# Attention over 32 memory slots, then a cosine feed-forward network: score and float32 fold products of 64x32 in two PSUM banks, the first batch's keys loaded ahead of its values, and a written order of issue

## The chip, the cores and the metric

The kernel runs on one core of a Trainium2 chip. The metric is the device time of one execution in microseconds. Before the change it is 708.84 us, the median of 3 runs (708.61 to 710.9).

## The reference

There are 8 batches of 576 tokens with 8 heads of 64. Per head, `phi` is turned by a softmax over the tokens into weights that gather keys and values into 32 memory slots; each token attends over the 32 slots; the heads side by side are a row of 512 that goes through the feed-forward network (4608 rows of 512, `w_in` 512 by 2048, `w_out` 2048 by 512).

```python
a = phi - np.max(phi, axis=2, keepdims=True)
a = np.exp(a)
a = a / (np.sum(a, axis=2, keepdims=True) + 1e-09)
k_m = np.einsum('bhsm,bhsd->bhmd', a, k)
v_m = np.einsum('bhsm,bhsd->bhmd', a, v)
scores = scale * np.matmul(q, k_m.transpose(0, 1, 3, 2))
scores = scores - np.max(scores, axis=-1, keepdims=True)
attn = np.exp(scores)
attn = attn / (np.sum(attn, axis=-1, keepdims=True) + 1e-09)
return np.matmul(attn, v_m).astype(np.float32)
...
h = x @ w_in
g = h * np.cos(h)
return (g @ w_out).astype(np.float32)
```

The weights come in as 64-bit floats and are turned into float32 on the chip.

## The kernel before

**Tiling.** The 4608 tokens are 12 groups of 384 (`GT`); two batches of 576 make three groups. The inner size 2048 is 16 chunks of 128 (`NF`). The main loop has 12 x 16 steps. In each, `gemm1` multiplies a chunk's folded weight with a group's attention rows into a PSUM tile `hp`; `act` and `act_end` make h*cos(h) of it on ScalarE and VectorE (L544 to L559); `gemm2` adds its product with the chunk of `w_out` to three PSUM tiles `acc`, four steps later (`LAG`).

**The attention is folded into the weights.** `x @ w_in` is attention times (`v_m` times `w_in`), so for each batch a *fold* multiplies `vm` (the 32 value slots of each head) with `w_in`, 256 rows by 2048 columns, and `gemm1` has an inner size of 256 in place of 512. `fold_first` (batch 0) and `fold` with `b < 2` (batch 1) do so in float32 from `w_in_sb`; from batch 2 on `fold_psum` uses half-precision high and low parts (`vp`, `vl`, `w2`), made in group 1.

**Precision.** Group 0 multiplies in float32 (L524, L572). From group 1 on each product is three half-precision ones, high x high, high x low and low x high (L533: 6 products of 384 columns, or 12 of 192 where a group spans two batches; L577: 9 of 512).

**Batch preparation.** `prep(b)` is `memory(b)` and then `attend(b)`, a generator advanced a step at a time beside the main loop. `memory` takes the softmax of `phi` and sums keys and values into `psA` (L270: 32-column tiles, `kv` chunks of at most 128 tokens with a column of ones for the denominators), divides (L283 to L287), turns the result around (`tpx`, L292) and copies it to `km` and `vm` (L299 to L302). Both are kept with zeros between two heads, filled by GpSimd, so one product of 128 rows by 64 columns serves two heads:

```python
nc.tensor.matmul(sc[D * p:D * (p + 1), g * n:(g + 1) * n], lhsT=km[:, 2 * g + p],
                 rhs=qt[:, 2 * g + p, t0:t0 + n], start=True, stop=True)
```

`attend` makes the scores in blocks of tokens (`BLK`: 256, 256, 64; batch 0: 256, 128, 192), one PSUM tile `sc` of the small pool a block (`score_products`), transposes each out on VectorE in 32x32 squares (`score_back`, L381), and takes the softmax (L389 to L400, the exponential on ScalarE, L422).

**PSUM.** Eight banks: three for `acc` (`ps_acc`), three for `hp` (`ps_h`), two for everything else (`ps_s`, `small_ps`): scores, folds, `psA`, `tpx`.

**The start.** Loads go out on SyncE's queue in program order: `phi`, all of batch 0's `kv`, the first 384 tokens of `q`, then the weight pieces (`load_w_in`, `load_w_out`). `to_float32` turns a piece into float32: VectorE takes the sign (L143), ScalarE the low exponent bits and a scaling (L147, L151), VectorE joins them (L152), ScalarE squares for the scale (L154). Between the first products stand `warm` products on zeros (L630), which nobody reads. During group 0 one piece is turned per step, and `fold_first` follows each piece of `w_in`.

**Order of issue.** A scheduler in the framework orders each engine's instructions from its own cost estimates; `tc.keep_in_program_order` pins single ones.

## Time and profile before

| | us |
|---|---|
| median of 3 runs | 708.84 (708.61 to 710.9) |
| the profiled execution | 710.08 |
| its span | 708.3 |
| mean granted TensorE clock | 0.994 of full speed |

The profiled execution is one run of its own; its span is what the rows of the profile cover. A row of the list of groups names the line, the engine, the operation, output <- input with their shapes and the count, then busy time and the mean of one instruction in ns, then the idle time just before them and what ended most of it. A timeline row has the start, the duration, the engine, the line and the operation, with the wait ahead of it in brackets. A product's tile is written rows*columns (128*64), its operands partitions x elements. In windows the rows have the window and its length, then each engine's busy time and instructions (TensorE's products, TensorE's weight loads, VectorE, ScalarE, GpSimd), the granted clock, the share of the DMA engines and GB/s.

### The profile page before, as it was taken

To read this page: it belongs to the slowest core of one execution; us is meant where nothing else is said; L and a number is where in the kernel's file an instruction comes from. 1 tells how busy PE (TensorE), PEld (TensorE's weight loads), DVE (VectorE), ACT (ScalarE), POOL (GpSimd) and SP (SyncE) were. 2 spreads that over 40 slices of the span, in tenths; PEclk is the share of its full clock that TensorE was granted. 3 is DMA by queue.
4 is the path that set the end of the run, shared out by engine and by line. 5 is a ranking of instruction groups with operands and counts; after the bars stand their busy time and mean duration, and the time that the engine had idled before them with its cause. 6 is when DMAs were issued, how large, how long until landed. Compare 5 with 4: busy or idle time off the path is not lost.

```text
span 708.3 us, 11822 instructions
## 1 busy us (share of the span) xinstructions
PE 687.8 (97%) x4597; PEld 364.7 (51%) x4597; DVE 532.7 (75%) x1135; ACT 518.7 (73%) x951; POOL 13.7 (2%) x34
## 2 busy tenths in 40 slices
...
GB/s 281 379 321 218 266 293 60 105 61 195 146 1 237 44 1 1 56 226 1 44 1 167 99 16 1 46 206 31 44 2 2 22 23 1 46 1 1 45 1 44
DMA packets 31959, 66.18 MB, mean 93 GB/s; under 512 B 2208, under 2 KB 12320, under 8 KB 31904
## 3 DMA queue, kind: packets, MB, share of 16 engines
...
## 4 chain that ended last, share of the span: by engine, by line
PE 60%; DVE 21%; ACT 16%; DMA 2%; issue 1%; ACTq 0%; POOL 0%; DVEq 0%; SPq 0%
PE acc L577 33%; PE hp L533 16%; DVE u L547 4%; ACT u L552 3%; DVE u L556 3%; DVE gp L559 3%; PE psA L270 3%; DVE vw L478 2%; PE sc L376 2%; PE pv L471 2%; ACT gp L558 2%; DMA phi<-in_phi 2%; DVE wo L191 2%; PE hp L524 1%; DVE w_in_parts L202 1%
## 5 line engine op out<-in xcount | busy, mean ns | idle before, releaser
L577 PE MATMUL acc<-wo,gp 128*128 128x512 f16 x1584 | 371.8, 379 | 1.2 <-DVE ob L589 0.7
L577 PEld LDWEIGHTS <-gp 128*128 128x128 f16 x1584 | 153.3, 98 | 162.6 <-issue 4.1
L533 PE MATMUL hp<-aT,vw 128*128 128x192 f16 (+1 forms) x1440 | 202.7, 284 | 1.0 <-DVE u L556 1.0
L533 PEld LDWEIGHTS <-vw 128*128 128x128 f16 x1440 | 128.3, 98 | 77.4 <-issue 17.5
L552 ACT ACTIVATE u<-u,quarter 128x384 f32<-128x384 f32 x192 | 116.7, 615 | 63.8 <-DVE u L547 62.9
L556 DVE SCALAR_TENSOR_TENSOR u<-hp,u 128x384 f32<-128x384 f32 x176 | 96.5, 553 | 60.6 <-ACT u L552 60.1
L544 ACT ACTIVATE gp<-hp,cu 128x192 int32<-128x192 f32 (+1 forms) x240 | 115.4, 492 | 28.1 <-PE hp L533 12.3
L547 DVE SCALAR_TENSOR_TENSOR u<-hp,cu,gp 128x192 f32<-128x192 f32 (+1 forms) x240 | 118.8, 503 | 21.9 <-ACT gp L544 21.5
L559 DVE TENSOR_TENSOR gp<-u,gp 128x384 f16<-128x384 f32 x176 | 96.4, 552 | 43.0 <-ACT gp L558 41.9
L558 ACT CAST gp<-u 128x384 f16<-128x384 f32 x176 | 88.8, 510 | 54.3 <-DVE u L556 53.0
L572 PE MATMUL acc<-wo,gp 128*128 128x512 f32 x96 | 45.1, 599 | 0.0
L478 DVE SCALAR_TENSOR_TENSOR vw<-pv,vw 128x512 f16<-128x512 f32 x48 | 31.5, 684 | 3.0 <-ACT vw L477 2.9
L524 PE MATMUL hp<-aT,vf 128*128 128x384 f32 x64 | 25.6, 533 | 7.9 <-DVE vf L497 3.1
L477 ACT ACTIVATE vw<-pv 128x512 f16<-128x512 f32 x48 | 26.8, 589 | 1.1 <-PE pv L471 0.9
L572 PEld LDWEIGHTS acc<-wo,gp 128*128 128x128 f32 x96 | 17.4, 190 | 17.8 <-issue 15.2
L601 ACT ACTIVATE ob<-acc,os 128x512 f32<-128x512 f32 x27 | 17.8, 682 | 9.6 <-PE acc L577 7.1
L524 PEld LDWEIGHTS hp<-aT,vf 128*128 128x128 f32 x64 | 12.2, 202 | 20.1 <-issue 4.3
L552 ACT ACT_TABLE_LOAD x17 | 21.8, 1283 | 0.3
L270 PE MATMUL psA<-kv,phi 128*32 128x129 f32 (+1 forms) x640 | 21.0, 275 | 0.7 <-ACT phi L260 0.5
L376 PE MATMUL sc<-q,km 128*64 128x256 f32 (+3 forms) x192 | 19.8, 342 | 1.6 <-DVE vw L478 1.2
L270 PEld LDWEIGHTS psA<-kv,phi 128*32 128x32 f32 (+1 forms) x640 | 16.4, 109 | 7.3 <-issue 3.3
L376 PEld LDWEIGHTS sc<-q,km 128*64 128x64 f32 x192 | 12.1, 140 | 12.0 <-issue 3.6
...
## 6 DMA issues: line engine op xcount, KB each, us to landing
...
```

The source lines that it names most:

```text
L270: nc.tensor.matmul(psA[32 * j:32 * (j + 1), g * KV:(g + 1) * KV], lhsT=a[:n, c, h * M:(h + 1) * M], rhs=kvs[c][:n, h * KV:(h + 1) * KV], s ...
L376: nc.tensor.matmul(sc[D * p:D * (p + 1), g * n:(g + 1) * n], lhsT=km[:, 2 * g + p], rhs=qt[:, 2 * g + p, t0:t0 + n], start=True, stop=True)
L478: nc.vector.scalar_tensor_tensor(out=vw[:, 1, g], in0=src, scalar=T, in1=vw[:, 0, g], op0=ALU.mult, op1=ALU.subtract)
L533: nc.tensor.matmul(hp[:, c0:c0 + n], lhsT=vw[:, wi, g, fo * P:(fo + 1) * P], rhs=aT[:, ai, g, c1:c1 + n], start=(k == 0), stop=(k == 5))
L544: ins = nc.scalar.activation(ni[:, c], hp[:, c], AF.Copy, scale=cu, bias=0.25)
L547: nc.vector.scalar_tensor_tensor(out=u[:, c], in0=hp[:, c], scalar=cu, in1=ni[:, c], op0=ALU.mult, op1=ALU.subtract)
L552: nc.scalar.activation(u, u, AF.Sin, scale=TWO_PI_BELOW, bias=quarter)
L556: nc.vector.scalar_tensor_tensor(out=u, in0=hp[:, :GT], scalar=2.0 ** -17, in1=u, op0=ALU.mult, op1=ALU.mult)
L558: nc.scalar.copy(gp[:, 0], u)
L559: nc.vector.tensor_tensor(out=gp[:, 1], in0=u, in1=gp[:, 0], op=ALU.subtract)
L572: nc.tensor.matmul(accs[grp][t], lhsT=gp[:, t * P:(t + 1) * P], rhs=wo[:, f + 1], start=(f == 0), stop=(f == NF - 1))
L577: nc.tensor.matmul(accs[grp][t], lhsT=gp[:, gi, t * P:(t + 1) * P], rhs=parts[:, wi], start=(f == 0 and gi == 0 and wi == 0), stop=(f == N ...
```

## The change

`km` and `vm` lose their zeros: 32 columns a head. A block of scores becomes eight products of 64 rows by 32 columns, four heads on rows 0 to 63 into one bank and four on rows 64 to 127 into another; the blocks become 288 and 288 tokens (batch 0: 384 and 192), and two transposes take a block out. The float32 folds get the same form (`fold_single`), and `fold_first` copies one bank on ScalarE and one on VectorE. For batch 0 the host lays out keys (with the ones) and values apart; `memory_first` loads keys ahead of `q` and the first weight piece, values behind it, and sums, turns and copies the keys before the values. There are 43 warm products (before: 51). `NEXT` is a table with the position, among the instructions not yet issued, of the next one on each engine; `issue_in_order` makes each engine keep it. The pins go.

```diff
+K1 = D + 1
...
-BLK = [(0, 256), (256, 256), (512, 64)]
-BLK_FIRST = [(0, 256), (256, GT - 256), (GT, S - GT)]
+BLK = [(0, 288), (288, 288)]
+BLK_FIRST = [(0, GT), (GT, S - GT)]
...
+NEXT = {
+    mybir.EngineType.PE: (
+        "0x16 2x2 0x16 1x8 0x11 8 16x3 0x19 1 2 3 0x4 4 0x29 18x2 0x20 1 0x3 2x6 0x3 7x2 0x3 1 19x2 2 0x5 1 "
...
+    mybir.EngineType.SP: (
+        "0x34 6x2 0 5x2 0x2 3 0 2 0x5 16 0 1 0x3 1 0x3 1 0x3 1 0x2 2 0x7 2x2 0x6 2x2 0x6 2x2 0x6 2x2 0x12 "),
+}
+
+
+def issue_in_order(tc):
+
+
+    traced = [i for i in tc.nc.cur_bb.bb.instructions if not type(i).__name__.startswith("BassTile")]
+    for engine, text in NEXT.items():
+        left = [i for i in traced if i.engine == engine]
+        last = None
+        for word in text.split():
+            at, _, times = word.partition("x")
+            for _ in range(int(times or 1)):
+                ins = left.pop(int(at))
+                if last is not None:
+                    tc.add_manual_dep(ins, last.name, mybir.DependencyInfo(
+                        mybir.DependencyClass.NoSync, mybir.DependencyReason.DATA), reason="issue order")
+                last = ins
+        assert not left, engine
...
+    def load_first(src, c0, c1):
+        if c0 == 0:
+            loads["kv", 0] = [ld.tile([P, H * KV], F32, tag="kv", name=f"kv_0_{c}", bufs=5) for c in range(5)]
+        for c, (s0, n) in enumerate(TCH):
+            nc.sync.dma_start(out=loads["kv", 0][c][:n, c0:c1], in_=src[s0:s0 + n])
...
+        psk = small_ps("psk")
+        for c in range(5):
+            products(psk, c, 0, K1)
+            yield
...
+        tpx = small_ps("tpx_k")
+        for g in range(2):
+            nc.tensor.transpose(tpx[:, g * P:(g + 1) * P], X[:, g], ident)
+        lo, hi = slice(0, D), slice(D, P)
+        tv = tpx[:, 0:HM].rearrange("p (c t m) -> p c t m", t=2, m=M)
+        km = wk.tile([P, NP, M], F32, tag="km", name=f"km_{b}", bufs=1)
+        nc.scalar.mul(km[lo], tv[lo, :, 0], 1.0 / math.sqrt(D))
+        nc.vector.tensor_scalar(out=km[hi], in0=tv[hi, :, 1], scalar1=1.0 / math.sqrt(D), scalar2=None, op0=ALU.mult)
+        st["km", 0] = km
+        psv = ps_acc.tile([P, DM], F32, tag="ps_acc", name="psv")
+        for c in range(5):
+            products(psv, c, H * K1, D)
+            if c == 2:
+                yield
+        X = wk.tile([P, 2, P], F32, tag="back", name="X_v", bufs=4)
+        for g in range(2):
+            nc.scalar.activation(X[:, g].rearrange("p (t d) -> p t d", t=2),
+                                 psv[:, g * D:(g + 1) * D].unsqueeze(1).broadcast_to([P, 2, D]), AF.Copy,
+                                 scale=den[:, g:g + 1])
+        tpx = ps_acc.tile([P, DM], F32, tag="ps_acc", name="tpx_v")
+        for g in range(2):
+            nc.tensor.transpose(tpx[:, g * P:(g + 1) * P], X[:, g], ident)
+        tv = tpx[:, 0:HM].rearrange("p (c t m) -> p c t m", t=2, m=M)
+        vm = wk.tile([P, NP, M], F32, tag="vm", name=f"vm_{b}")
+        nc.scalar.copy(vm[hi], tv[hi, :, 0])
+        nc.scalar.copy(vm[lo], tv[lo, :, 1])
+        st["vm", 0] = vm
...
-        km = wk.tile([P, NP, 2 * M], F32, tag="km", name=f"km_{b}", bufs=1)
-        vm = wk.tile([P, NP, 2 * M], F32, tag="vm", name=f"vm_{b}")
-        nc.gpsimd.memset(km, 0.0)
-        nc.gpsimd.memset(vm, 0.0)
+        km = wk.tile([P, NP, M], F32, tag="km", name=f"km_{b}", bufs=1)
+        vm = wk.tile([P, NP, M], F32, tag="vm", name=f"vm_{b}")
         tv = tpx[:, 0:HM].rearrange("p (c t m) -> p c t m", t=2, m=M)
         lo, hi = slice(0, D), slice(D, P)
-        nc.scalar.mul(km[lo, :, 0:M], tv[lo, :, 0], 1.0 / math.sqrt(D))
-        nc.scalar.mul(km[hi, :, M:2 * M], tv[hi, :, 1], 1.0 / math.sqrt(D))
-        nc.vector.tensor_copy(out=vm[hi, :, 0:M], in_=tv[hi, :, 0])
-        nc.vector.tensor_copy(out=vm[lo, :, M:2 * M], in_=tv[lo, :, 1])
+        nc.scalar.mul(km[lo], tv[lo, :, 0], 1.0 / math.sqrt(D))
+        nc.scalar.mul(km[hi], tv[hi, :, 1], 1.0 / math.sqrt(D))
+        nc.vector.tensor_copy(out=vm[hi], in_=tv[hi, :, 0])
+        nc.vector.tensor_copy(out=vm[lo], in_=tv[lo, :, 1])
...
-            sc_at[i] = sc = small_ps(f"sc_{b}_{t0}")
-            for g in range(2):
-                for p in range(2):
-                    nc.tensor.matmul(sc[D * p:D * (p + 1), g * n:(g + 1) * n], lhsT=km[:, 2 * g + p],
-                                     rhs=qt[:, 2 * g + p, t0:t0 + n], start=True, stop=True)
+            sc_at[i] = sc = [small_ps(f"sc_{b}_{t0}_{g}") for g in range(2)]
+            for c in range(NP):
+                for g in range(2):
+                    rows = slice(g * D, (g + 1) * D)
+                    nc.tensor.matmul(sc[g][M * c:M * (c + 1), :n], lhsT=km[rows, c],
+                                     rhs=qt[rows, c, t0:t0 + n], start=True, stop=True)
 
         def score_back(i):
             t0, n = BL[i]
-            nc.vector.transpose(at[:, 2 * t0:2 * (t0 + n)], sc_at[i][:, :2 * n])
+            for g in range(2):
+                nc.vector.transpose(at[:, 2 * t0 + g * n:2 * t0 + (g + 1) * n], sc_at[i][g][:, :n])
...
-        score_products(0)
-        score_products(1)
-        score_back(0)
-        score_back(1)
-        yield
-        score_products(2)
-        score_back(2)
+        scores(0)
+        yield
+        scores(1)
...
     def fold_psum(b, q, g):
         pv = small_ps(f"pv_{b}_{q}_{g}")
-        for i in range(2):
-            c = 2 * g + i
-            if b < 2:
-                nc.tensor.matmul(pv[D * i:D * (i + 1)], lhsT=st["vm", b][:, c],
-                                 rhs=w_in_sb[:, c, q * FS:(q + 1) * FS], start=True, stop=True)
-        if b >= 2:
-            for first in (True, False):
-                for j in range(4):
-                    c, o = 2 * g + j // 2, 1 - j % 2
-                    nc.tensor.matmul(pv[M * j:M * (j + 1)], lhsT=(st["vp", b] if first else vl)[:, c, o],
-                                     rhs=st["w2", q][:, c, o], start=first, stop=not first, skip_group_check=True)
+        for first in (True, False):
+            for c in range(NP):
+                nc.tensor.matmul(pv[M * c:M * (c + 1)], lhsT=(st["vp", b] if first else vl)[:, c, 1 - g],
+                                 rhs=st["w2", q][:, c, 1 - g], start=first, stop=not first, skip_group_check=True)
+        return pv
+    def fold_single(b, name, c0, n):
+        pv = [small_ps(f"{name}_{g}") for g in range(2)]
+        for c in range(NP):
+            for g in range(2):
+                rows = slice((1 - g) * D, (2 - g) * D)
+                nc.tensor.matmul(pv[g][M * c:M * (c + 1), :n], lhsT=st["vm", b][rows, c],
+                                 rhs=w_in_sb[rows, c, c0:c0 + n], start=True, stop=True)
         return pv
...
-        for g, pv in enumerate([fold_psum(b, q, g) for g in range(2)]):
-            split_fold(b, vw, g, pv)
+        pv = fold_single(b, f"pv_{b}_{q}", q * FS, FS) if b < 2 else [fold_psum(b, q, g) for g in range(2)]
+        for g in range(2):
+            split_fold(b, vw, g, pv[g])
 
     def fold_first(j):
         q, r = divmod(j, 2)
         if r == 0:
             st["vf", q] = wk.tile([P, 2, FS], F32, tag="vw", name=f"vf_{q}", bufs=8)
-        pv = small_ps(f"pvf_{j}").rearrange("p (g x) -> p g x", g=2)
-        for g in range(2):
-            for i in range(2):
-                c = 2 * g + i
-                nc.tensor.matmul(pv[D * i:D * (i + 1), g], lhsT=st["vm", 0][:, c],
-                                 rhs=w_in_sb[:, c, j * WS:(j + 1) * WS], start=True, stop=True)
-        (nc.scalar.copy if j < 2 else nc.any.tensor_copy)(out=st["vf", q][:, :, r * WS:(r + 1) * WS], in_=pv)
+        pv = fold_single(0, f"pvf_{j}", j * WS, WS)
+        nc.scalar.copy(out=st["vf", q][:, 0, r * WS:(r + 1) * WS], in_=pv[0][:, 0:WS])
+        nc.vector.tensor_copy(out=st["vf", q][:, 1, r * WS:(r + 1) * WS], in_=pv[1][:, 0:WS])
...
-    load_kv(0)
+    load_first(k_first, 0, H * K1)
     load_q(0)
     load_w_in(0)
+    load_first(v_first, H * K1, H * KV)
...
-        warm((1, 1, 2, 2, 0)[c])
+        if c < 4:
+            warm(1)
     next(mem)
     warm(3)
-
-    def attention_rest(sign):
-        tc.keep_in_program_order(sign)
-        next(mem)
-        warm(2)
-
-    convert_w_in(0, attention_rest)
-    for _ in mem:
-        pass
+    next(mem)
+    convert_w_in(0)
     first = attend(0)
     next(first)
-    warm(12)
+    warm(4)
+    next(mem)
+    warm(2)
+    next(mem)
+    next(mem)
+    warm(2)
     fold_first(0)
     warm(6)
     next(first)
+    for _ in mem:
...
+        pass
...
+    issue_in_order(tc)
...
+        "k_first": np.concatenate([kt[0], np.ones((S, H, 1), k.dtype)], axis=2).reshape(S, H * K1),
+        "v_first": np.ascontiguousarray(vt[0]).reshape(S, H * D),
```

Three places show what the table and the rest move. First TensorE at batch 2's scores, late in group 1: `sc_2_0` and the like are score blocks of batch 2 (after: with the bank's number behind), `acc_1` and `hp_2` are main products of groups 1 and 2, `32x288 x4` are four products into a 32-row strip each. Before, the first two blocks and, 28 rows on, the third:

```order
L577 LDWEIGHTS gp_1_13_1395
L577 MATMUL acc_1_2_1032<-wo_87,gp_1_13_1395 128x512
L376 MATMUL sc_2_0_1633<-q_2_659,km_2_1587 64x256 x4
L376 MATMUL sc_2_256_1638<-q_2_659,km_2_1587 64x256 x4
L533 LDWEIGHTS vw_1_0_780
```

```order
L577 MATMUL acc_1_2_1032<-wo_87,gp_1_14_1431 128x512
L577 LDWEIGHTS gp_1_14_1431
L577 MATMUL acc_1_2_1032<-wo_87,gp_1_14_1431 128x512
L376 MATMUL sc_2_512_1669<-q_2_659,km_2_1587 64x64 x4
L533 LDWEIGHTS vw_1_0_780
```

and after the change:

```order
L749 MATMUL acc_1_1_1133<-wo_87,gp_1_14_1541 128x512
L556 MATMUL sc_2_0_0_1741<-q_2_741,km_2_1697 32x288 x4
L749 LDWEIGHTS gp_1_14_1541
L749 MATMUL acc_1_2_1134<-wo_87,gp_1_14_1541 128x512
L556 MATMUL sc_2_0_1_1742<-q_2_741,km_2_1697 32x288 x4
L749 LDWEIGHTS gp_1_14_1541
L749 MATMUL acc_1_2_1134<-wo_87,gp_1_14_1541 128x512
L749 LDWEIGHTS gp_1_14_1541
L749 MATMUL acc_1_2_1134<-wo_87,gp_1_14_1541 128x512
L556 MATMUL sc_2_288_0_1777<-q_2_741,km_2_1697 32x288 x4
L707 LDWEIGHTS vw_1_0_874
```

The first block's two banks now stand apart, with a product of group 1 between them, and one bank of the second block follows after two more.

Then VectorE at the start, from the division of batch 0's sums on: `den`, `X` and `l1` are of `memory`, `at`, `rm` and `rs` of the first score blocks, `w_in_sb`, `raw_in` and `wo` of the weight pieces. Before:

```order
L283 TENSOR_SCALAR den_0_203<-psA_0_156 128x2
L284 RECIPROCAL den_0_203<-den_0_203 128x2
L287 TENSOR_SCALAR X_0_206<-psA_0_156,den_0_203 128x128 x2
L306 TENSOR_REDUCE l1_0_230<-X_0_206 128x4
L308 TENSOR_TENSOR l1_0_230<-l1_0_230,vmask_78 128x4
L310 TENSOR_REDUCE l2_0_233<-l1_0_230 128x1
L301 COPY vm_0_217<-tpx_0_213 64x4x32
L302 COPY vm_0_217<-tpx_0_213 64x4x32
L164 TENSOR_SCALAR ev_0_237<-l3_0_235 128x1
L165 TENSOR_SCALAR ev_0_237<-ev_0_237 128x1
L381 STREAM_TRANSPOSE at_0_241<-sc_0_0_244 128x512
L381 STREAM_TRANSPOSE at_0_241<-sc_0_256_250 128x256
```

and after:

```order
L253 TENSOR_SCALAR w_in_sb_86<-raw_in_0_106 128x4x256
L375 TENSOR_SCALAR den_0_206<-psk_161 128x2
L376 RECIPROCAL den_0_206<-den_0_206 128x2
L379 TENSOR_SCALAR X_k_209<-psk_161,den_0_206 128x128 x2
L259 SCALAR_TENSOR_TENSOR w_in_sb_86<-raw_in_0_106,w_in_sb_86 128x4x256
L390 TENSOR_SCALAR km_0_218<-tpx_k_215 64x128
L562 STREAM_TRANSPOSE at_0_227<-sc_0_0_0_230 128x384
L562 STREAM_TRANSPOSE at_0_227<-sc_0_0_1_231 128x384
L570 TENSOR_REDUCE rm_0_228<-at_0_227 128x24
L571 TENSOR_TENSOR at_0_227<-at_0_227,rm_0_228 128x768
L253 TENSOR_SCALAR w_in_sb_86<-raw_in_1_113 128x4x256
L575 TENSOR_REDUCE rs_0_229<-at_0_227 128x24
```

The first piece's sign (L253, before L143) has moved ahead of the division and its join (L259, before L152) ahead of the copy of `km`; the values' part (`l1`, `vm`) has left the stretch ahead of the scores.

Last ScalarE at the start, from its first weight piece on. Before (`km` is copied ahead of it, `vf` are copies of folds):

```order
L299 ACTIVATE km_0_216<-tpx_0_213 64x4x32
L300 ACTIVATE km_0_216<-tpx_0_213 64x4x32
L147 ACTIVATE w_in_sb_86<-raw_in_0_106 128x4x256
L151 ACTIVATE raw_in_0_106<-raw_in_0_106 128x1024
L422 ACTIVATE at_0_241<-at_0_241 128x768
L147 ACTIVATE w_in_sb_86<-raw_in_1_108 128x4x256
L154 ACTIVATE raw_in_0_106,sq_90<-w_in_sb_86 128x1024
L497 COPY vf_0_268<-pvf_0_269 128x2x256
```

and after:

```order
L257 ACTIVATE w_in_sb_86<-raw_in_0_106 128x4x256
L258 ACTIVATE raw_in_0_106<-raw_in_0_106 128x1024
L389 ACTIVATE km_0_218<-tpx_k_215 64x128
L261 ACTIVATE raw_in_0_106,sq_90<-w_in_sb_86 128x1024
L257 ACTIVATE w_in_sb_86<-raw_in_1_113 128x4x256
L400 ACTIVATE X_v_289<-psv_246,den_0_206 128x128
L603 ACTIVATE at_0_227<-at_0_227 128x768
L400 ACTIVATE X_v_289<-psv_246,den_0_206 128x128
L258 ACTIVATE raw_in_1_113<-raw_in_1_113 128x1024
L408 COPY vm_0_295<-tpx_v_292 64x128
L409 COPY vm_0_295<-tpx_v_292 64x128
```

The first piece (L257, before L147) now comes ahead of `km`, its square (L261, before L154) ahead of the exponential, and the values' products are divided and copied here (L400, L408, L409).

125 lines of the change are left out of this document (81 added, 44 removed), and 74 rows, old and new, of the table NEXT.

## The prediction

> **What bounds the kernel now.** I read the page first, then busy time by stage, then single stretches of TensorE's timeline. The page's first lines, and the three narrow product groups that the change rewrites:
>
> ```profile
> span 708.3 us, 11822 instructions
> PE 687.8 (97%) x4597; PEld 364.7 (51%) x4597; DVE 532.7 (75%) x1135; ACT 518.7 (73%) x951; POOL 13.7 (2%) x34
> L577 PE MATMUL acc<-wo,gp 128*128 128x512 f16 x1584 | 371.8, 379 | 1.2 <-DVE ob L589 0.7
> ```
> ```profile
> L376 PE MATMUL sc<-q,km 128*64 128x256 f32 x120 | 14.7, 385 | 0.3 <-POOL l L312 0.3
> L495 PE MATMUL pvf<-w_in_sb,vm 128*64 128x256 f32 x64 | 9.6, 422 | 2.2 <-DVE w_in_sb L152 2.1
> L465 PE MATMUL pv<-w_in_sb,vm 128*64 128x512 f32 x32 | 7.7, 605 | 0.0
> ```
>
> TensorE is busy 97% of the span, but that is an average over two stages. Busy time by stage (the window, its length, then PE, PEld, DVE, ACT, POOL):
>
> ```profile
> 18.70:110.00 91.30, 81.19 (x371) 39.27 (x368) 77.85 (x150) 87.10 (x123) 1.99 (x6) 0.96 0.82 282
> 110.00:150.00 40.00, 39.27 (x234) 21.38 (x233) 39.81 (x82) 37.91 (x78) 0.31 (x1) 1.00 0.29 74
> 150.00:250.00 100.00, 99.33 (x733) 53.22 (x731) 89.32 (x198) 78.39 (x144) 2.71 (x6) 1.00 0.39 121
> 250.00:350.00 100.00, 99.19 (x748) 55.60 (x747) 72.10 (x162) 71.01 (x142) 2.37 (x5) 1.00 0.17 58
> 350.00:450.00 100.00, 98.38 (x660) 50.43 (x659) 72.24 (x150) 68.63 (x127) 2.87 (x4) 1.00 0.15 50
> 450.00:550.00 100.00, 99.99 (x793) 55.53 (x791) 75.64 (x177) 73.06 (x141) 2.09 (x4) 1.00 0.18 59
> 550.00:650.00 100.00, 99.82 (x669) 55.13 (x668) 70.33 (x144) 70.51 (x140) 0.00 (x0) 1.00 0.05 17
> ```
>
> Up to 110 us ScalarE sets the pace: 87.1 of 91.3 us busy, 4.2 idle. From 150 us on it is TensorE: 500 us long, idle for 0.67+0.81+1.62+0.01+0.18 = 3.3 us in all. In that stage a microsecond of TensorE work is a microsecond of time, and 3.3 us is about all that a better order can win back.
>
> **TensorE's prices** come from its timeline (start, duration, what):
>
> ```profile
> 468.67 0.40 PE L471 MATMUL pv<-w_in_sb,vl 128*32 128x512 f16 x4
> 469.00 1.16 PE L533 MATMUL hp<-aT,vw 128*128 128x192 f16 x12
> 470.00 1.03 PE L577 MATMUL acc<-wo,gp 128*128 128x512 f16 x4
> 471.04 1.95 PE L376 MATMUL sc<-q,km 128*64 128x256 f32 x16
> 472.92 1.25 PE L577 MATMUL acc<-wo,gp 128*128 128x512 f16 x5
> 474.10 0.45 PE L376 MATMUL sc<-q,km 128*64 128x64 f32 x8
> 474.49 1.16 PE L533 MATMUL hp<-aT,vw 128*128 128x192 f16 x12
> 475.49 2.11 PE L577 MATMUL acc<-wo,gp 128*128 128x512 f16 x9
> 477.43 1.15 PE L533 MATMUL hp<-aT,vw 128*128 128x192 f16 x12
> ```
>
> Durations overlap, so I take start to start. Nine full-width products of 512 half-precision columns take 477.43-475.49 = 1.94 us, 0.216 each. A float32 product is two records, and each record of 256 columns streams as long: four logical products per block, two 64-column halves side by side, two blocks, so 8 rounds of 0.216 = 1.73 us. The row says 1.88 (471.04 to 472.92): 0.15 goes at leaving. The five products ahead of the second visit take 1.18 instead of 5 x 0.216 = 1.08: 0.10 goes at entering. So each visit of TensorE to a narrow shape costs about 0.25 us beside its streaming. The start shows the same for the very shape that the change brings, 64 rows by 32 columns:
>
> ```profile
> 14.11 0.61 PE L630 MATMUL warm<-zeros 128*128 128x512 f16 x2
> 14.65 0.64 PE L270 MATMUL psA<-kv,phi 64*32 64x129 f32 x16
> 15.22 0.82 PE L630 MATMUL warm<-zeros 128*128 128x512 f16 x3
> ```
>
> From 14.11 to 15.22 is 1.11 us: two warm products (0.43), 16 records of 129 columns on four column tiles (4 rounds of 0.216 x 129/256 = 0.109, so 0.44), and 0.24 for the visit.
>
> **Scores.** If all eight 64x32 products of a block run side by side, a block of 288 columns is two records of 0.243, 0.49 us, and a batch 0.97 in two visits, 1.47 with them. Before it is 1.88 + 0.39 (474.10 to 474.49) + two entries of 0.10 = 2.46. For the six batches 2 to 7, which lie in TensorE's stage, blocks kept whole would save 6 x 0.99 = 5.9 us. But the table does not keep them whole. Counted in the order listing from the first product of group 1 to the end, the scores of batches 2 to 7 make 20 visits (before: 12), each one round of 0.49, since no visit holds a tile twice: 20 x (0.49 + 0.25) = 14.8, against 6 x 2.46 = 14.8 before. **The scores save nothing.** In batch 5 the second block alone makes three visits, of one, two and five products.
>
> **Folds.** Batch 1's last three float32 folds: before, 3 visits of 2 rounds of 0.86 (512 columns, two records of 0.43): 3 x (1.73+0.25) = 5.9. After, 7 visits of one round: 7 x (0.86+0.25) = 7.8, so +1.9. The half-precision folds keep their products, but their visits rise from 25 to 31: +1.5, and one fold cut 5 to 11 adds a round of 0.22. Sum in TensorE's stage: 0 + 1.9 + 1.7 = **+3.6 us**. The bounds: +3.6 - 18 x 0.25 = -0.9 if more visits cost nothing (46 become 64), which the 64x32 row above speaks against; the upper end is the second rival. I take +3.6, since both rows agree on the price.
>
> **The start.** ScalarE's first weight piece waits for its load:
>
> ```profile
> 18.71 1.37 ACT L147 ACTIVATE w_in_sb<-raw_in 128x1024 int16<-128x1024 uint8 x1 [1.12 <-DMA raw_in<-in_w_in]
> 20.52 1.15 ACT L151 ACTIVATE raw_in<-raw_in 128x1024 f32<-128x1024 f32 x1 [0.44 <-DVE w_in_sb L143]
> 22.34 0.84 ACT L422 ACTIVATE at<-at 128x768 f32<-128x768 f32 x1 [0.67 <-DVE at L390]
> 23.09 1.36 ACT L147 ACTIVATE w_in_sb<-raw_in 128x1024 int16<-128x1024 uint8 x1
> 24.30 1.13 ACT L154 ACTIVATE raw_in<-w_in_sb 128x1024 f32<-128x1024 f32 x1
> 0.00:10.00 10.00, 8.14 (x27) 3.47 (x28) 3.45 (x14) 1.35 (x2) 1.01 (x7) 1.00 0.73 252
> 10.00:20.00 10.00, 9.33 (x118) 4.69 (x116) 4.48 (x16) 3.30 (x6) 0.35 (x1) 1.00 1.05 333
> L497 ACT COPY vf<-pvf 128x512 f32<-128x512 f32 x4 | 2.3, 574 | 0.0
> L260 ACT ACTIVATE phi<-phi 64x256 f32<-64x256 f32 x2 | 0.8, 400 | 0.0
> L299 ACT ACTIVATE km<-tpx 64x128 f32<-64x128 f32 x2 | 0.5, 272 | 5.6 <-PE tpx L292 5.6
> L552 ACT ACT_TABLE_LOAD x17 | 21.8, 1283 | 0.3
> 107.87 1.15 PE L533 MATMUL hp<-aT,vw 128*128 128x192 f16 x12
> ```
>
> With v (576 x 2048 bytes = 1.18 MB) behind it, that piece lands 1.18 / 0.333 = 3.5 us earlier, near 15.2 (a DMA share of 1.05 in the row says the queues are full, so bytes set the time). The second piece has the same bytes ahead of it as before, and in the new order ScalarE reaches it after only L147, L151 (with its 0.44 of waiting), km and L154 of the first, 15.2 + 1.4 + 1.6 + 0.3 + 1.1 = 19.6 at the earliest. Before, it was taken at 23.09 without a wait, so it landed between 18.7 and 23.1. The loads ahead of it and its own are 5.9 MB by their shapes; the first 10 us moved 2.5 (252 GB/s), and the other 3.4 at 333 GB/s take 10.2 us, so it lands near 20.2 or a little later. So 1 us or so of the 3.5 becomes a new wait. ScalarE also gets work: eight copies of 256 fold columns (0.40 by the L260 row) for four of 512 (574 ns) +0.9, X_v and vm four small ones of 0.27 +1.1, less one km and one short piece of aT, -0.5: +1.5 us. Left: 3.5 - 1 - 1.5 = 1 us, between -1.5 and +2.5. The attention chain does not run ahead of this. On VectorE the first piece's sign (L143) now stands ahead of den, and its join (L152) ahead of the half of km that the second row half needs, and the transposes back wait behind four operations on later pieces. I take 0.5 us gained, and leave the eight fewer warm products and the memsets gone from GpSimd (13.7 us busy in all, hidden) at nothing. Two more table loads on ScalarE (36 for 34) fall where it is 70% busy: nothing, or 2 x 1.28 = 2.6 us if that cover were gone. Group 1, where TensorE's stage begins, is the row at 107.87.
>
> **The order itself.** It can win back at most 4.2 us of ScalarE's idle time at the start and 3.3 us of TensorE's. The rows show no way to tell how much; both kernels issue in a fixed order, and every added visit makes TensorE later than its neighbours, which closes gaps. I take a quarter, 1.7 us.
>
> **Sum.** +3.6 - 0.5 - 1.7 = +1.4 us. The profiled execution took 710.08 us with a span of 708.3, 1.8 us around it; the median shown is 708.84, 1.24 less than that execution. Changes carry over, so 708.84 + 1.4 = **710.2 us**, 711.5 against the profiled one. A measurement of this kernel can tell about 0.3%, 2.1 us, from no change.
>
> **Rivals.**
>
> 1. *The order pays more than the visits cost.* All 4.2 and 3.3 us of idle time go and the start gives 1: 3.6 - 8.5 = -4.9, so 703.9; two thirds of it gives 706.8. For it: VectorE and ScalarE have a quarter of their time free after 150 us. Against it: the visits.
>
> 2. *The row halves do not run side by side.* No row of the trace shows two row halves at once: the 64-row products of L270 all lie on rows 0 to 63. Then a block held whole takes as long as its longest column's queue, and because products are issued column by column with both halves in turn, the second half of each column holds up the next column: up to five rounds in place of one. About ten of the 20 score visits hold both halves: 10 x 0.49 = 4.9 more if only columns queue, four times that, 19.6, if issue is held up, and one fold visit 0.9: +6 to +20, so 716 to 730. A rule of the Trainium skill bears on it: TensorEngine Tiling (Array Packing), Tiling Modes, says of tiles that "Different tiles can execute LdWeights and Matmul in parallel". By it this rival gives nothing and the sum stays +3.6; without it the sum is that plus 6 to 20. What the trace shows for column tiles (the 16 records of 129 columns above in 4 rounds) agrees with it, and no run here shows it for rows.
>
> 3. *A new wait on PSUM banks*, which ends slower. The small pool has two banks. Before, a score block took one; now it takes both, and the next block cannot begin until VectorE has transposed out of the first's. Already before, the third block waited:
>
> ```profile
> 474.10 0.31 PEld L376 LDWEIGHTS sc<-q,km 128*64 128x64 f32 x8 [0.42 <-DVE at L381]
> L381 DVE STREAM_TRANSPOSE at<-sc 128x512 f32<-128x512 f32 x15 | 10.5, 705 | 0.5 <-PE sc L376 0.5
> ```
>
> A transpose of 288 columns costs near 705 x 288/512 = 0.4 us. In batch 2 one half of a block ends and its bank is wanted again after one wide product, a half block, two wide products and the visits, some 1.5 us later; VectorE must be through by then, and with two operations as long as that transpose ahead of it in its queue it is not. From that point each block costs up to 1.2 us: six batches, +7, so with +1.4 it is 717. The same skill page warns of it (Restrictions and Gotchas: row tiling raises PSUM pressure).
>
> **Chances.** The forecast, within 707 to 713: 0.40. First rival: 0.25. Second: 0.11. Third: 0.24. Faster by over 0.3% (under 706.7): most of the first rival and a little of the forecast, 0.26. Slower by over 0.3% (over 711.0): the second, the third and a quarter of the forecast, 0.42. Within: 0.32. The range leaves out the far end of the first rival and the second's beyond 718, about 0.15 in all: 704 to 718.
>
> **What would show it.** Right, if the new profile has score visits of about 0.49 + 0.25 us, one round each whatever number of products they hold; if the 256-column products of fold_first do so too; if TensorE stays over 99% busy from 150 us on; and if the first L147 starts near 15 us and the second waits. Wrong, if a visit of eight products takes over 0.8 us (second rival), if TensorE's weight loads wait for L562's transposes by more than 0.5 us a batch (third), or if group 1 starts well before 107 us with ScalarE's gaps closed (first). The sum itself is wrong if entering and leaving 64x32 costs other than 0.25 us.

## The result

The changed kernel takes **722.46 us** (median of 4 runs, 721.9 to 723.11), the kernel before 709.87 us beside it (4 runs, 708.61 to 710.99): ratio 1.0173, 95% interval 1.0148 to 1.0197. The forecast was 710.2 us with a range of 704 to 718. The change costs 12.6 us where 1.4 were expected.

### The profile page after: what moved, and what is told of

It is laid out like the page before. It is cut to its first block, busy times and chain, and to the rows that moved or that the text cites. A ratio compares the mean times of both kernels' runs of the same rounds, so it can differ in the third digit from the quotient of the medians.

```text
span 720.6 us, 12291 instructions
## 1 busy us (share of the span) xinstructions
PE 702.8 (98%) x4829; PEld 353.5 (49%) x4829; DVE 529.8 (74%) x1129; ACT 520.4 (72%) x954; POOL 9.1 (1%) x18
## 4 chain that ended last, share of the span: by engine, by line
PE 79%; ACT 11%; DVE 6%; DMA 2%; issue 1%; ACTq 0%; SPq 0%; DVEq 0%
PE acc L749 42%; PE hp L707 21%; PE acc L744 3%; PE pv L639 3%; PE hp L698 2%; PE psA L454 2%; PE sc L556 2%; PE pv L648 2%; PE pvf L648 1%; ACT u L724 1%; ACT gp L718 1%; DMA raw_in<-in_w_in 1%; ACT L724 1%; DVE u L719 1%; PE warm L803 1%
## 5 line engine op out<-in xcount | busy, mean ns | idle before, releaser
L749 PEld LDWEIGHTS <-gp 128*128 128x128 f16 x1584 | 150.9, 98 | 176.1 <-issue 18.4
L707 PE MATMUL hp<-aT,vw 128*128 128x192 f16 (+1 forms) x1440 | 199.0, 283 | 2.5 <-DVE u L728 1.1
L718 ACT ACTIVATE gp<-hp,cu 128x192 int32<-128x192 f32 (+1 forms) x240 | 113.9, 491 | 69.0 <-PE hp L707 52.0
L719 DVE SCALAR_TENSOR_TENSOR u<-hp,cu,gp 128x192 f32<-128x192 f32 (+1 forms) x240 | 117.1, 503 | 45.0 <-ACT gp L718 43.8
L724 ACT ACTIVATE u<-u,quarter 128x384 f32<-128x384 f32 x192 | 115.0, 612 | 44.3 <-DVE u L719 39.7
L744 PE MATMUL acc<-wo,gp 128*128 128x512 f32 x96 | 47.9, 613 | 0.0
L744 PEld LDWEIGHTS acc<-wo,gp 128*128 128x128 f32 x96 | 16.4, 189 | 21.4 <-issue 19.6
L724 ACT ACT_TABLE_LOAD x18 | 23.1, 1283 | 0.3
L556 PE MATMUL sc<-q,km 64*32 64x288 f32 (+2 forms) x256 | 21.0, 434 | 2.4 <-DVE at L562 1.0
L454 PE MATMUL psA<-kv,phi 128*32 128x129 f32 (+1 forms) x560 | 17.8, 275 | 0.3 <-DVE vw L655 0.3
L454 PEld LDWEIGHTS psA<-kv,phi 128*32 128x32 f32 (+1 forms) x560 | 14.5, 109 | 4.8 <-issue 3.1
L803 PE MATMUL warm<-zeros 128*128 128x512 f16 x43 | 15.7, 525 | 1.2 <-DVE vmask L167 1.2
```

What stands on the lines that cost most here:

```text
L454: nc.tensor.matmul(psA[32 * j:32 * (j + 1), g * KV:(g + 1) * KV], lhsT=a[:n, c, h * M:(h + 1) * M], rhs=kvs[c][:n, h * KV:(h + 1) * KV], s ...
L556: nc.tensor.matmul(sc[g][M * c:M * (c + 1), :n], lhsT=km[rows, c], rhs=qt[rows, c, t0:t0 + n], start=True, stop=True)
L707: nc.tensor.matmul(hp[:, c0:c0 + n], lhsT=vw[:, wi, g, fo * P:(fo + 1) * P], rhs=aT[:, ai, g, c1:c1 + n], start=(k == 0), stop=(k == 5))
L718: nc.scalar.activation(ni[:, c], hp[:, c], AF.Copy, scale=cu, bias=0.25)
L719: nc.vector.scalar_tensor_tensor(out=u[:, c], in0=hp[:, c], scalar=cu, in1=ni[:, c], op0=ALU.mult, op1=ALU.subtract)
L724: nc.scalar.activation(u, u, AF.Sin, scale=TWO_PI_BELOW, bias=quarter)
```

## The profile after

The page's first lines and two groups, with the columns of before, and then the durations (min/median/max in ns, first and last start) of the folds' line:

```profile
span 720.6 us, 12291 instructions
PE 702.8 (98%) x4829; PEld 353.5 (49%) x4829; DVE 529.8 (74%) x1129; ACT 520.4 (72%) x954; POOL 9.1 (1%) x18
...
L749 PE MATMUL acc<-wo,gp 128*128 128x512 f16 x1584 | 372.7, 379 | 0.4 <-ACT ob L773 0.3
...
L556 PE MATMUL sc<-q,km 64*32 64x288 f32 (+2 forms) x256 | 21.0, 434 | 2.4 <-DVE at L562 1.0
```
```profile
L648 PE MATMUL pvf<-w_in_sb,vm x128: 372/400/632, 28.3 to 102.9; 64*32 64x256 f32 x128
...
L648 PE MATMUL pv<-w_in_sb,vm x64: 589/601/613, 102.6 to 159.0; 64*32 64x512 f32 x64
```

TensorE's share went up, from 97 to 98%, while the kernel became slower: "busy" counts narrow visits and products at half clock as well. Where the time went is seen when both spans are cut where a group's first `hp` product starts. First before, then after (window, length, PE, PEld, DVE, ACT, POOL, granted clock, DMA share, GB/s); the windows are start, group 0, group 1, group 2, the rest:

```profile
0.00:27.00 27.00, 21.86 (x166) 9.96 (x166) 14.76 (x41) 10.51 (x14) 1.36 (x8) 1.00 0.93 316
27.00:107.90 80.90, 73.39 (x321) 35.24 (x322) 67.73 (x131) 77.84 (x113) 1.99 (x6) 0.96 0.82 279
107.90:164.70 56.80, 56.06 (x352) 32.41 (x352) 56.58 (x117) 53.42 (x110) 0.31 (x1) 1.00 0.33 80
164.70:224.70 60.00, 59.41 (x478) 31.70 (x477) 51.21 (x123) 43.82 (x78) 2.40 (x5) 1.00 0.44 142
224.70:708.30 483.60, 477.02 (x3286) 255.37 (x3284) 342.42 (x728) 333.10 (x640) 7.65 (x14) 1.00 0.13 46
```
```profile
0.00:34.80 34.80, 27.94 (x248) 10.41 (x248) 17.49 (x41) 15.71 (x22) 0.54 (x5) 0.80 0.97 332
34.80:114.40 79.60, 76.41 (x395) 30.58 (x395) 64.17 (x128) 72.88 (x107) 1.14 (x2) 0.98 0.72 246
114.40:175.30 60.90, 59.54 (x379) 32.13 (x378) 56.97 (x119) 54.97 (x112) 0.78 (x1) 1.00 0.28 66
175.30:240.00 64.70, 62.96 (x502) 30.65 (x500) 54.19 (x126) 49.86 (x85) 0.70 (x2) 1.00 0.45 140
240.00:720.60 480.60, 475.91 (x3314) 249.77 (x3310) 336.96 (x719) 326.97 (x631) 5.94 (x8) 1.00 0.13 46
```

Group 1 begins 6.5 us later, groups 1 and 2 take 4.1 and 4.7 us more, the other nine 3.0 less. So half of the loss is there before TensorE's stage begins. More still: at that point 28 records of group 0's own `acc` products (L744) are yet to come, before the change 24 (L572), and these four cost 2.1 us behind it. Two more things are in these rows: the granted clock of the start is 0.80 where it was 1.00, and in group 1 of before VectorE is busy for 56.58 of 56.80 us, so that group was never TensorE's alone.

**The start after**, ScalarE's and VectorE's timeline (start, duration, instruction, the wait ahead of it):

```profile
14.50 1.35 ACT L257 ACTIVATE w_in_sb<-raw_in 128x1024 int16<-128x1024 uint8 x1 [2.98 <-DMA raw_in<-in_w_in]
...
18.11 1.14 ACT L261 ACTIVATE raw_in<-w_in_sb 128x1024 f32<-128x1024 f32 x1 [1.14 <-DVE w_in_sb L259]
...
20.98 1.36 ACT L257 ACTIVATE w_in_sb<-raw_in 128x1024 int16<-128x1024 uint8 x1 [1.66 <-DMA raw_in<-in_w_in]
...
25.57 0.37 ACT L400 ACTIVATE X_v<-psv,den 128x128 f32<-128x128 f32 x1 [3.23 <-PE psv L365]
25.83 0.83 ACT L603 ACTIVATE at<-at 128x768 f32<-128x768 f32 x1
...
33.37 0.37 ACT L670 COPY vf<-pvf 128x256 f32<-128x256 f32 x1 [1.33 <-PE pvf L648]
```
```profile
14.50 0.75 DVE L253 TENSOR_SCALAR w_in_sb<-raw_in 128x1024 int16<-128x1024 int8 x1 [3.63 <-DMA raw_in<-in_w_in]
15.15 0.14 DVE L375 TENSOR_SCALAR den<-psk 128x2 f32<-128x2 f32 x1
...
21.63 0.96 DVE L571 TENSOR_TENSOR at<-at,rm 128x768 f32<-128x768 f32 x1
...
26.70 0.95 DVE L575 TENSOR_REDUCE rs<-at 128x24 f32<-128x768 f32 x1 [3.44 <-ACT at L603]
...
33.82 1.03 DVE L587 STREAM_TRANSPOSE aT<-at 128x384 f32<-128x384 f32 x2
```

and TensorE's timeline and granted clock there:

```profile
13.56 0.80 PE L365 MATMUL psk<-kv,phi 128*32 128x65 f32 x32
16.02 0.50 PE L385 MATMUL tpx_k<-ident,X_k 128*128 128x128 f32 x2 [1.66 <-DVE X_k L379]
17.03 2.93 PE L556 MATMUL sc<-q,km 64*32 64x384 f32 x16 [0.51 <-ACT km L389]
...
34.78 1.65 PE L698 MATMUL hp<-aT,vf 128*128 128x384 f32 x2
```
```profile
18.00:24.00 6.00, 5.95 (x66) 2.31 (x63) 4.12 (x7) 2.57 (x3) 0.00 (x0) 0.50 1.05 383
...
28.00:36.00 8.00, 7.24 (x26) 2.33 (x27) 6.38 (x14) 6.64 (x9) 0.35 (x1) 0.50 1.06 376
```

It is a chain of queues. The sums `psk` are done at 14.36. But in VectorE's fixed order the first piece's sign (L253) stands ahead of the division (L375), and its load lands at 14.50, so the division starts at 15.15. TensorE idles from 14.36 to 16.02 (before, three warm products filled most of this stretch), and its granted clock falls to 0.50. The `psv` sums, with eight warm products between them, end at 25.5; the half clock is a small part of that, for with the clock mostly up (e3, below) ScalarE's `X_v` starts only 0.7 us earlier. It (L400) waits 3.23 us for them with the exponential (L603) queued behind, whose input was ready at 22.59 (21.63 + 0.96). VectorE waits for that exponential 3.44 us, the transposes back end the chain at 34.8, and only then can group 0's products begin. From its first weight piece to group 1, a window of before and one of after:

```profile
18.70:107.90 89.20, 79.09 (x357) 37.71 (x354) 75.75 (x144) 85.00 (x120) 1.99 (x6) 0.96 0.84 289
```
```profile
14.50:114.40 99.90, 92.03 (x526) 35.78 (x527) 77.48 (x152) 85.77 (x124) 1.49 (x3) 0.91 0.79 271
```

ScalarE is idle for 99.9 - 85.8 = 14.1 us in place of 89.2 - 85.0 = 4.2.

**TensorE from group 1 on**, visit by visit: a fold, one score product alone, and a block of scores held whole:

```profile
157.78 0.81 PE L749 MATMUL acc<-wo,gp 128*128 128x512 f16 x3
158.53 1.06 PE L648 MATMUL pv<-w_in_sb,vm 64*32 64x512 f32 x8
159.52 2.76 PE L749 MATMUL acc<-wo,gp 128*128 128x512 f16 x12
...
233.97 1.47 PE L749 MATMUL acc<-wo,gp 128*128 128x512 f16 x6
235.37 0.67 PE L556 MATMUL sc<-q,km 64*32 64x288 f32 x2
235.97 1.47 PE L749 MATMUL acc<-wo,gp 128*128 128x512 f16 x6
...
484.90 2.54 PE L749 MATMUL acc<-wo,gp 128*128 128x512 f16 x11
487.37 0.72 PE L556 MATMUL sc<-q,km 64*32 64x288 f32 x16
488.02 0.82 PE L749 MATMUL acc<-wo,gp 128*128 128x512 f16 x3
```

Eleven wide products are 11 x 0.216 = 2.38, the rows say 2.47: 0.09 for entering. From 487.37 to 488.02 is 0.65: all eight score products of a block, both row halves, in one round of 0.49, and 0.16 for leaving. Such a visit costs 0.74. The one product alone, two records, is 0.60 in place of the 0.65. The fold is 0.10 + 0.99 = 1.09. Not every block held whole is as cheap: those that start at 483.02 and 560.83 take 0.97 and 0.88.

Taken over all of TensorE's timeline from group 1 on, with the full-width half-precision products at their price (514.5 us in every kernel), this is what the rest goes to, in us, visits in brackets. A wait ahead of or in the middle of a visit is counted with it (in e18 some 1.1 us in batch 2's scores). The lines "without waits" leave these out, and "all waits" has them in. What is missing to the stretch is the time after the last product. e2 and e18 are experiments below; the stretch is from group 1's first product to the end of the span:

| | before | after | e2 | e18 |
|---|---|---|---|---|
| scores | 16.15 (12) | 15.82 (20) | 15.02 (15) | 11.31 (12) |
| without waits | 14.9 | 15.1 | 13.5 | 10.8 |
| float32 folds, float32 products of group 0 | 16.31 | 20.00 | 14.44 | 17.24 |
| folds alone, without waits | 5.8 (3) | 7.4 (7) | 4.4 (4) | 3.3 (3) |
| group 0's products alone (records) | 10.5 (24) | 12.6 (28) | 9.7 (22) | 13.9 (28) |
| half-precision folds | 26.67 (25) | 27.58 (31) | 28.04 (26) | 27.91 (31) |
| without waits | 26.3 | 27.6 | 26.7 | 27.3 |
| sums, their turns, maxima | 19.91 | 19.56 | 20.53 | 19.57 |
| waits between products | 2.65 | 4.70 | 5.27 | 5.92 |
| all waits | 5.0 | 5.9 | 9.6 | 7.6 |
| stretch | 600.44 | 606.17 | 602.06 | 600.47 |

## The experiments

All kernels are timed beside the kernel before on the same chip, which was at 709.49 to 710.55 us there. "Group 1" is the start of its first product in the profiled execution, "rest" the time from there to the end of its span; before these are 107.87 and 600.44, after 114.41 and 606.17. A profiled execution is one of several: that of e18 (712.98) and that of e9 (712.37) were the slowest of theirs.

| run | us | ratio (95%) | group 1 | rest |
|---|---|---|---|---|
| e1, no table | 722.1 | 1.0170 (1.0139 to 1.0201) | 108.02 | 609.94 |
| e2, products alone | 711.85 | 1.0025 (1.0012 to 1.0038) | 107.28 | 602.06 |
| e3, warm products | 720.8 | 1.0155 (1.0128 to 1.0182) | 111.76 | 606.18 |
| e5, whole scores | 718.94 | 1.0128 (1.0100 to 1.0156) | 114.12 | 603.52 |
| e6, start by hand | 723.39 | 1.0189 (1.0172 to 1.0206) | 115.52 | 606.25 |
| e7, e6 and whole visits | 716.95 | 1.0107 (1.0086 to 1.0129) | 113.58 | 601.66 |
| e8, e1 with the pins | 715.66 | 1.0085 (1.0070 to 1.0100) | 108.02 | 605.79 |
| e9, before with batch 1's folds | 710.65 | 1.0004 (0.9993 to 1.0015) | 108.76 | 601.82 |
| e10, before with the scores | 715.04 | 1.0066 (1.0046 to 1.0087) | 108.86 | 602.47 |
| e11, e2 with a third bank | 721.8 | 1.0163 (1.0145 to 1.0181) | 110.96 | 609.39 |
| e12, before with a third bank | 722.33 | 1.0169 (1.0155 to 1.0184) | 113.65 | 606.31 |
| e13, before with less ScalarE | 713.17 | 1.0047 (1.0034 to 1.0060) | 111.18 | 599.42 |
| e14, VectorE free | 746.43 | 1.0512 (1.0489 to 1.0536) | 125.83 | 621.12 |
| e15, ScalarE free | 768.29 | 1.0829 (1.0800 to 1.0857) | 122.36 | 643.15 |
| e16, TensorE free | 729.86 | 1.0287 (1.0263 to 1.0310) | 112.15 | 617.86 |
| e17, start free | 717.31 | 1.0100 (1.0078 to 1.0122) | 108.66 | 606.81 |
| e18, start free, whole visits | 711.11 | 1.0010 (0.9993 to 1.0026) | 110.72 | 600.47 |
| e19, e18 and pinned warm products | 711.87 | 1.0018 (1.0008 to 1.0028) | 110.22 | 599.94 |

### The parts: the order, the products

**e1** leaves the order to the scheduler; **e8** has the old pins back as well; **e2** is the kernel before with the new products, layout and blocks alone, its own loads, pins and scheduler.

```diff
...
-    issue_in_order(tc)
```

> The changed kernel without the table: the framework's scheduler orders every engine again; loads, products, banks and warm products are those of the change. Theory A (the written order lost the time: at the start it lets TensorE go idle so that its clock halves, and puts ScalarE's exponential behind the division of the values; later it cuts scores and folds into 64 narrow visits): the order listing now has 53 visits after the start of group 1, 4 fewer of scores (0.715 us each), 4 fewer of float32 folds (1.09), 4 fewer of half-precision folds (0.46), so 9 us less there, and some 4 to 6 us less at the start: 707 to 710 us, no window under 0.9 of the clock before 30 us. Theory B (the new form itself loses it: keys and values apart, two banks a block): 718 us or more, clock halved at 17 to 25 us as before.

> The kernel before with only the 64x32 products (scores and float32 folds, two banks a block, blocks of 288, two copies a fold); loads, start and scheduler as before. Theory A (a visit costs 0.25 us beside its streaming, row halves stream side by side): 15 score visits of 0.715 = 10.7 us for 16.1 before, 4 float32 fold visits of 1.09 = 4.4 for 5.9, one more half-precision visit +0.25: 7 us less than before, 702 to 705 us. Theory C (two banks a block hold up the next block and the folds, since the pool has no third): 709 us or more, with waits of TensorE on the transposes of over 0.5 us a batch.

> e1_no_table with the pins of the kernel before put back (warm products, second piece's sign and start, the subtraction from batch 4 on, the first operation of some steps). Theory G (the pins, not the form, are what e1_no_table lost against e2_products, 10.3 us; the table stands in for them): stage from group 1 to the end 602 to 604 us, 711 to 714 us. Theory B (keys and values apart cost it, with any order): 719 us or more.

Without the table the time hardly moves, 722.1 us, but it lies elsewhere: group 1 begins 6.4 us earlier and all that follows takes 3.8 longer. (Its profiled execution, 718.0 us of span, is faster than its median.) With the pins 715.7. The new products alone cost 1.5 us: the table above has them 1.1 us cheaper in scores and 1.9 in float32 work, with 1.4 more in half-precision folds (most of it waits inside visits) and 2.6 more in waits between products. Of the 1.9, 0.9 is not a saving: two records fewer of group 0 lie behind group 1's start. With all waits taken out, scores and folds are 2.4 us cheaper and all waits 4.7 us longer. In e1 and e8 keys come first and group 1 still begins no earlier than before, at 108.0. Less of group 0 is left to do there (22 and 18 records of its `acc` products for 24), but that does not reach the time: e8, which is e2 with the new start, takes 3.8 us more than e2. So the new start, earlier keys and all, bought no time in the scheduler's order either.

### The clock and the start's order

**e3** sets 15 more warm products about TensorE's gap, in TensorE's table too, to keep the clock up; **e6** also puts the start of the table, on three engines, in an order by hand (division ahead of the first piece's sign, exponential ahead of the first piece's square).

```diff
...
     next(mem)
-    warm(3)
+    warm(18)
```

> The changed kernel with 15 more warm products (7 ahead of the keys' turning, 3 ahead of the values' turning, 5 ahead of the first fold), every order else kept. Theory D (the idle TensorE halved its own clock, and the values' sums, the warm products and the first folds at half speed are what ScalarE and VectorE then wait for): granted clock 1.00 from 17 to 30 us, ScalarE's wait for the values' sums falls from 3.23 us to under 1.5, the first product of group 0 starts 3 to 5 us earlier than 34.8, and the time is 717 to 719.5 us. Theory E (the order of ScalarE and VectorE alone holds it up): clock back, but the first product of group 0 at 33.5 us or later, and 721 us or more.

> e3_clock with the first rows of three tables altered as well: on TensorE the first scores, the values' sums and the first fold each in a row, and the warm products in the waits between them; on ScalarE the values' division ahead of the first piece's square, the exponential no longer behind a wait for a later load; on VectorE the keys' division ahead of the first piece's sign, and sums, normalising and turning back of the first block ahead of the second piece's join. Theory F (besides the halved clock it is this order that delays the first product of group 0): that product starts at 24 to 27 us (e3_clock: 32.2), ScalarE's idle time between the first piece and group 1 falls by 4 to 6 us, 715 to 717 us. Rival (group 0 is held by later waits, as in e1_no_table, where its first product at 25.5 brought group 1 no earlier than before): group 1 starts within 1 us of e3_clock's 111.8, 719.5 us or more.

In e3 the clock is at half from 19.7 to 23.1 us alone, where after has it at half from 17.2 to 24.0 and from 27.4 to 37.7. Group 1 comes 2.65 us earlier and the time falls by 1.7 to 720.8: the clock is part of it, not most. e6 refutes the theory that an earlier first product of group 0 is what is missing. There it starts at 27.59, 7.2 us earlier than after, and group 1 at 115.52, later still. The order behind the repaired stretch had not been changed with it, and the wait only moved: a few products on, a fold waits 6.89 us. The row names VectorE's `ev` (38.92) as what ended it; just ahead of that, at 38.59, VectorE copies the fold before out of its bank, behind four operations on weight pieces and a step of h*cos(h):

```profile
39.15 1.78 PE L646 MATMUL pvf<-w_in_sb,vm 64*32 64x256 f32 x8 [6.89 <-DVE ev L269]
```

**e13** asks whether ScalarE alone sets the start: the squares of four `w_out` pieces go to VectorE, in the kernel before (there as the square of the largest value, not the sum of squares).

```diff
...
-        to_float32(wo[:, 2 * j + 1:2 * j + 3], loads.pop(("out", j)), sq[:, 1, j:j + 1])
+        to_float32(wo[:, 2 * j + 1:2 * j + 3], loads.pop(("out", j)), sq[:, 1, j:j + 1], on_vector=j in (2, 4, 6, 7))
```

> The kernel before with the squares of four of the eight pieces of w_out (third, fifth, seventh, eighth) taken from ScalarE: VectorE takes the largest magnitude of the piece and squares that one number a row, so the scale of the second product is set from a largest square in place of a sum of squares for them. Theory K (from its first piece of weights to group 1 ScalarE alone sets the time: busy 85.0 plus idle 4.2 of 89.2 us): ScalarE does 4 x 1.3 = 5.3 us less up to group 1, its idle time grows by 1 to 3 us, group 1 starts at 104 to 106 us (before 107.9), and the time is 706 to 708.5 us. Rival L (VectorE sets it as much: it idles 13.4 us in that stretch and gets 5.6 more): group 1 at 107 us or later, 709.5 or more.

Group 1 came 3.3 us later, not earlier, and the whole is 2.8 us slower. ScalarE's busy time to group 1 did not even fall (86.2 us in its window, before 85.0): the scheduler gave it 4.9 us of group 1's work on weights in place of the squares. So the run does not show what a shorter ScalarE would do under an unchanged order; it does show that work moved from the busiest engine to the next one was no time won.

### How the engines' orders hang together

**e14**, **e15** and **e16** take one engine out of the table, VectorE, ScalarE or TensorE.

```diff
 NEXT = {
...
-    mybir.EngineType.DVE: (
...
```

> The changed kernel with VectorE's row taken out of the table: the scheduler orders VectorE, the other engines keep their written order. Theory M (VectorE's order costs the start: the first piece's sign, which waits for its load, stands ahead of the keys' division, and signs and joins of later pieces ahead of normalising): group 1 starts at 110 us or before (the changed kernel: 114.4), 716 to 719 us. Rival: under 1.5 us from the changed kernel, since VectorE then waits for the others' order.

> The changed kernel with ScalarE's row taken out of the table, the others kept. Theory N (ScalarE's order costs the start: the exponential behind the values' division, 3.2 us): exponential at 22.5 to 23 us (25.8), group 1 at 111 us or before, 717.5 to 719.5 us. Rival: under 1.5 us from the changed kernel, since VectorE's written order puts the second piece and the values' sums ahead of what the earlier exponential would allow.

> The changed kernel with TensorE's row taken out of the table, the others kept. Theory D (TensorE's order costs the start: warm products packed ahead of the keys' last sums, so that it idles, its clock halves, and values' sums and first folds are late): granted clock 1.00 up to 22 us at least, group 1 at 111 us or before; later 67 narrow visits in place of 64, so the stage from group 1 on is 0 to 2 us longer than 606.2; 718 to 721 us. Rival (the other engines' written order holds the start): group 1 at 113 us or later, 722 us or more.

Each is slower, by 24, 46 and 7 us against the 722.46. In e15 the waits come up on engines that are not freed; the main products' groups (the last columns: idle time just before them, what ended most of it) of after and of e15:

```profile
L707 PE MATMUL hp<-aT,vw 128*128 128x192 f16 (+1 forms) x1440 | 199.0, 283 | 2.5 <-DVE u L728 1.1
```
```profile
L688 PE MATMUL hp<-aT,vw 128*128 128x192 f16 (+1 forms) x1440 | 202.6, 286 | 14.9 <-DVE u L709 11.9
L730 PE MATMUL acc<-wo,gp 128*128 128x512 f16 x1584 | 377.8, 382 | 12.0 <-DVE gp L712 7.2
```

That the scheduler's guess for one engine does not fit the other two, which cannot give way, is how I read it; no run shows it apart. Either way the order can't be tried out engine by engine. **e17** frees all three, but only until about group 1:

```diff
+FREE = {mybir.EngineType.PE: 345, mybir.EngineType.Activation: 114, mybir.EngineType.DVE: 177}
...
-        last = None
+        last, free = None, FREE.get(engine, 0)
...
-                if last is not None:
+                free -= 1
+                if last is not None and free < 0:
```

> The changed kernel with the table holding TensorE, ScalarE and VectorE only from the start of group 1 on (after 345, 114 and 177 instructions); up to there the scheduler orders all three together. Theory P (the start's 6.5 us are the written order's, all engines together): group 1 at 108 to 110 us as in e1_no_table, the stage after it 606 us as in the changed kernel: 714.5 to 717.5 us. Rival B (keys ahead of values cost it, in any order): group 1 at 112 us or later, 720 us or more.

Group 1 at 108.66, 5.75 us earlier than after, the rest as after (606.81), the time 5.1 us less. That isolates the table's order in the start: it costs 5.1 of the 12.6 us. What is left against before is group 1's 0.8 us and four more records of group 0 behind it (28 for 24). The new products alone (e2) do not have that, so it lies with keys first and the fewer warm products, although the first piece is there 3.5 us earlier (15.17): ScalarE's idle time from there to group 1 is 9.0 us in place of 4.2. No run parts the two.

### The visits

**e5** issues the score blocks of batches 2 to 7 whole on TensorE, 12 visits for 20, the rest of the table as it is. **e7** is e6 with whole scores, batch 1's float32 folds whole and one cut half-precision fold joined; **e18** is the same visits with e17's free start. Only the table's numbers differ; two of TensorE's lines that stand in the same place, in after and in e18:

```diff
...
-        "0x3 4x12 1 0x3 1 15 0 1x12 0 15 2x12 0 1 0 22 0x16 7 8 0x7 2 0x3 12x3 15x3 33x3 0x12 3x15 0x3 21x3 "
+        "2x12 0 1 0x31 12x3 15x3 33x3 0x12 3x15 0x3 21x3 0x15 24x3 0x3 21x8 15x3 36 0x3 12x3 0x12 12x6 0x12 2 "
```

> The changed kernel with TensorE's table alone altered: each score block of batches 2 to 7 has its eight products in a row, at the place of its last one; 12 visits in place of 20. Theory A (each visit costs its 0.5 us of streaming and 0.25 for entering and leaving, whatever it holds): 8 x 0.715 = 5.7 us less, 716 to 717.5 us. Theory C (the block waits for its banks, so the time comes back as a wait): 720 us or more, visits of eight products over 1.2 us from wide product to wide product.

> e6_start with whole visits: the eight products of each score block of batches 2 to 7 and of each float32 fold of batch 1 in a row, and one half-precision fold that was cut rejoined; 52 visits after the start of group 1 in place of 64. Theory A with the part that e5_scores gave back (8 score visits fewer: 3.0 us; 4 float32 fold visits fewer: 4.4 us, two thirds of it kept): 5 to 6 us less than e6_start. Theory C (whole blocks want both banks at once): within 2 us of e6_start.

> e17_free_start with the whole visits of e7_whole in the rest of the table (52 narrow visits after the start of group 1 in place of 64). Theory A with P: the stage from group 1 to the end as in e7_whole, 601.7 us, so 4 to 5 us less than e17_free_start: 710 to 713 us, level with the kernel before or up to 3 us behind it. Theory C: within 2 us of e17_free_start.

Whole scores take 11.32 us where the split ones take 15.82: 4.5 less, of which 2.65 reach the stretch and 3.5 the time. With the folds whole too the stretch is 601.66 in e7 and 600.47 in e18, that of the kernel before. e18 is level with before (interval 0.9993 to 1.0026): the best of the changed kernels, and no gain. Against e17 the whole visits are worth 6.2 us. So the start's order (5.1, after to e17) and the cut visits (6.2, e17 to e18) are 11.3 of the 12.6 us. Against before, e18's scores are 4.8 us cheaper, and 3.3 come back as waits between products, 1.2 in six more visits of half-precision folds and 0.9 in float32 work. That last figure holds two: the folds are 2.5 us cheaper, and 3.4 us more of group 0's own products lie behind group 1's start.

**e19** adds twelve warm products to e18, pinned ahead of group 0's first product, against the clock's fall there.

```diff
-    warm(6)
+    warm(18, pin=True)
```

> This is the free start with whole visits and twelve more warm products, pinned into the free start's order on TensorE between group 0's last fold and its first narrow product, so that TensorE has no stretch of idle time there. What it tells apart: whether what is left between that kernel and the one before (711.1 against 709.5 us) is TensorE's halved clock in the start. If it is: the granted clock is 1.00 from 24 to 32 us, group 1 begins at 108 to 109.5 us where it was 110.7, and the time is 708.5 to 710 us, level with before or up to 1 us under it, with less spread than 708.1 to 713. The rival, that group 0's length is set by ScalarE and VectorE whatever the clock is: group 1 stays within 1 us of 110.7 and the time within 1 us of 711.1.

TensorE's timeline and two windows of e18, then of e19:

```profile
26.07 4.18 PE L698 MATMUL hp<-aT,vf 128*128 128x384 f32 x6 [3.27 <-DVE aT L587]
```
```profile
24.00:28.00 4.00, 1.93 (x3) 1.18 (x4) 3.71 (x6) 1.14 (x1) 0.00 (x0) 0.50 1.05 386
...
40.00:44.00 4.00, 1.17 (x33) 0.32 (x18) 2.73 (x7) 4.00 (x8) 0.00 (x0) 1.00 1.02 340
```
```profile
23.21 6.42 PE L803 MATMUL warm<-zeros 128*128 128x512 f16 x18
29.46 0.81 PE L698 MATMUL hp<-aT,vf 128*128 128x384 f32 x2
```
```profile
24.00:28.00 4.00, 4.00 (x11) 1.49 (x10) 3.71 (x6) 2.59 (x3) 0.00 (x0) 0.50 1.04 385
...
40.00:44.00 4.00, 4.00 (x13) 2.59 (x10) 2.54 (x5) 2.81 (x4) 0.00 (x0) 0.50 1.01 347
```

The products did not keep the clock up: it had fallen before they began, and they ran at half speed themselves for most of their time (6.42 us; at 0.216 they would be 3.9). So the clock's share in e18 stays open. What the run does show is that group 0's first product moved 3.4 us later, to 29.46, and group 1 not at all (110.22 and 110.72): where group 1 begins is not set by when TensorE begins group 0.

### The banks

**e9** and **e10** put one of the two products into the kernel before: batch 1's float32 folds (`vm` of batch 1 on without zeros), or the scores (`km` without zeros, blocks of 288, one buffer of `rm`).

> The kernel before with only the four float32 folds of batch 1 as 64x32 products (two banks, as those folds had before); all else as before. The folded rows of batch 1 then stand in another order than its attention's, so that batch's output isn't the reference's. Theory A: same visits (3 after the start of group 1, 46 in all), each 1.09 us in place of 1.96: 3 x 0.87 = 2.6 us less, 707 to 708 us. Theory C (narrow products give nothing back, as in e2_products): within 1 us of before.

> The kernel before with only the scores as 64x32 products in two banks a block (blocks of 288; one small tile kept single to make room); folds as before, so the attention's rows stand in another order than the folds' and the output isn't the reference's. Theory A: 14 visits of 0.715 = 10.0 us for 16.1: 705 to 707 us even with one us of waits. Theory C (each block takes both banks, so it waits for the transposes of the one ahead and holds up the folds): the 6 us come back as waits, 709 us or more.

**e11** and **e12** move one PSUM bank from `hp` to the small pool, in e2 and in the kernel before, so that a score block of two banks has one to spare.

```diff
-    ps_h = ctx.enter_context(tc.tile_pool(name="ps_h", bufs=3, space=PSUM))
-    ps_s = ctx.enter_context(tc.tile_pool(name="ps_s", bufs=2, space=PSUM))
+    ps_h = ctx.enter_context(tc.tile_pool(name="ps_h", bufs=2, space=PSUM))
+    ps_s = ctx.enter_context(tc.tile_pool(name="ps_s", bufs=3, space=PSUM))
```

> e2_products with a third bank for scores and folds, taken from the first products' pool (2 banks in place of 3). Theory C (banks): waits of scores and half-precision folds fall by 2 us or more against e2_products; what the first products lose for their bank is seen in e12_banks. So e11 minus e12 is below e2 minus before (+1.5 us) by 2 us or more. Rival (the scheduler's order, not the banks): the difference stays +1 to +2.

> The kernel before with the same banks as e11_banks (three small, two for the first products), as its control. Every theory: slower than before, since the first products of the next step wait for a bank; 711 to 725 us.

e9 is level: its folds are 2.55 us cheaper in group 1 and after, and its waits between products are 2.9 us more. Part of that is VectorE's share in group 1, seen above: TensorE idles there for 2.05 of 55.9 us, before for 0.74 of 56.8, while VectorE is busy for 55.39 of them. So 1.3 us of the saving is waited away at once; the other waits come later, on VectorE and ScalarE. e10, whose rows of folds and attention no longer match (it is for its time alone), is 4.7 us slower by the ratio, more than e2 which contains its change; the two are ordered by the scheduler, each in its own way, and why they differ so was not settled. With a third small bank the new products are 0.5 us ahead of the old ones (721.8 and 722.33), where with two they are 1.5 behind. That speaks for the banks as the price of 64x32, but 2 us between kernels that the scheduler orders afresh is not proof, and the bank is missed more by `hp`, whose third one it was. TensorE's waits from group 1 on (total, times, longest) in before, in e12 and in e11:

```profile
PE hp L533 <- DVE u L556: 1.0, 2, 0.8
```
```profile
PE hp L533 <- DVE u L556: 5.3, 9, 1.5
```
```profile
PE hp L526 <- DVE u L549: 10.9, 16, 2.3
```

## Why the prediction was wrong

The prices of the visits were right to within a microsecond, and the forecast fell by two other terms, the start above all. Term by term, forecast and measured:

- **Visits of scores: nothing** (14.8 against 14.8). Measured -0.3 us (15.82 against 16.15), without waits +0.2 (15.1 against 14.9), 20 visits as counted. That split blocks give away the gain is shown by e5 and e18.
- **Folds: +1.9 and +1.7.** Measured +1.6 for the float32 folds (7.4 against 5.8) and +1.3 without waits (+0.9 with them) for half precision. A float32 visit is 1.09 (worked out 1.11). The float32 line of the table rises by 3.7, but 2.1 of that are the four records of group 0, which belong to the start. All narrow work without waits and without these is +2.9, with the sums' -0.2; forecast +3.6.
- **"The order itself": -1.7.** Wrong in sign. Waits between products rose from 2.65 to 4.70, +2.05; all waits from 5.0 to 5.9, +1.0. That is a miss of 2.7 to 3.8 us. The sign that TensorE stays over 99% busy from 150 us on came true (497.2 of 500 us from 150 to 650) and proved nothing, since busy time counts cut visits too. The step took idle time as something that a written order could only fill. That a fixed order is only as good as the durations it was fitted to is argued, not shown.
- **The start: -0.5.** This is the step that failed most: group 1 came 6.5 us later, a miss of 7.0, and with 2.1 us more of group 0's work still to do. Its first half held: the first piece was taken at 14.50, 4.2 us earlier (forecast 3.5), ScalarE's work is 0.8 us more (forecast 1.5), and the second piece waited (1.66; forecast "1 us or so"). What was not priced is waiting through the queues. The prediction named the moved instructions, the sign ahead of `den`, the transposes behind the pieces, and then "I take 0.5 us gained", as if ScalarE could go on with pieces meanwhile. In a fixed order it could not: idle time of ScalarE is 14.1 us, not 4.2, and e17, with the order of the start set free, brings group 1 back to 108.66. And "the eight fewer warm products ... at nothing" left out the clock; e3, with most of it back, is 2.65 us earlier at group 1.

In sum, 2.9 of narrow work, 1.0 of all waits, 2.1 of group 0's products and 6.5 of start make 12.5 of 12.3 us of span (the rest, -0.2, is the time after the last product).

- **The first rival** (the order pays) is refuted by the same figures: the written order cost time. **The second**, row halves that do not run side by side, gave 716 to 730, a range that holds the measured time by accident: the row at 487.37 refutes it. The sign named for it, a visit of eight products over 0.8 us, did occur (0.97 and 0.88), but in two of five visits, far from the 2.5 us of five rounds, and the other three take 0.74. The Trainium skill, TensorEngine Tiling (Array Packing), Key Properties, says that different tiles run in parallel; for rows the trace now agrees, 16 records of 288 columns in one round of 0.49 us. **The third**, banks, gave 717: from group 1 on the score products wait for no transpose (L562), and their weight loads once, for 0.4 us, so in the written order it is not there. In the scheduler's order e11 and e12 leave it open.
